# Sending the normalised rows of one more batch to columns through DRAM, and building a parity mask from the identity, in a fused attention and gated MLP kernel

## The chip, the cores and the metric

The kernel runs on one core of one Trainium2 chip. The metric is the time on the device in microseconds (us), and the number that stands for a kernel is the median of its runs. Four runs of the kernel before are known: 311.81, 311.83, 313.54 and 314.72 us, median 312.69 us. One execution was taken by the hardware profiler; its own time is 311.81 us, and the span from its first to its last instruction is 310.1 us. The granted TensorE clock was 1.0 over the whole span.

Engines are written as the profile writes them: PE is TensorE (matrix products), DVE is VectorE, ACT is ScalarE, POOL is GpSimd, SP is SyncE, whose queue here issues DMAs and nothing else.

## The reference, cut to what matters

```python
B, H, S, D = 8, 8, 576, 64                        # float32 inputs
scores = q @ k.T / sqrt(D)                        # per batch and head
rel = pos[:, None] - pos[None, :]
plain = (rel >= 0) & (rel < 32)                   # heads 0 to 3
dil = (rel >= 0) & (rel < 128) & (rel % 4 == 0)   # heads 4 to 7
attn = softmax(where(mask, scores, -1e9)) @ v
x = attn.transpose(0, 2, 1, 3).reshape(4608, 512) # a row per token
h = x @ w_in                                      # 512 -> 2048
g = h * sigmoid(beta * h)                         # beta: one number per column
out = g @ w_out                                   # 2048 -> 512, float32
```

Attention is narrow: a query sees 32 keys, either its neighbours (plain heads) or every fourth position behind it (dilated heads). Nearly all the arithmetic is in the two big products of the MLP.

## The kernel before, in words

**The MLP.** The 4608 tokens are cut into 9 tiles of 512. For each tile and each of 16 blocks of 128 hidden columns, `slot_h` makes h with four products (L818), each 128x128 weights by up to 512 tokens; ACT takes a tanh of it (L825) and DVE gates it into `g_t` (L830), of which there are two, used in turn. `block` then makes 128 rows of the output with 16 products over `g_t` and `w_out_bf` (L850); ACT or DVE brings them from PSUM to `osb` (L867, L869; four buffers), and SP stores them (L875). A tile is 64 products of each kind. Tile 0 has its first four blocks cut in two at token 288, so it has 80 of L818.

**What a tile of the MLP needs.** L818 reads `xT`, the attention output with features down the partitions and tokens along the columns. Tile 0 reads batch 0's tokens alone, in two halves; tile 1 batches 0 and 1; tile 2 (tokens 1024 to 1535) needs both halves of batch 2, and tile 3 batches 2 and 3.

**Attention of one batch.** The steps have names, in the order of the strings FIRST and LATER (L157, L158): KD0 to QP1 turn k and q to columns by PE transposes (L427, L434; only for batches below DIRECT = 3, later ones come transposed by DMA, L417); S2, S3 are scores of the dilated heads (L638), T those of the last 16 positions of each residue, the tail (L612), S00 to S11 those of the plain heads (L672 or L697). ACT takes exponentials (L580) and POOL or DVE multiply by 0/1 masks (L584). In batch 0 most masks are added by PE instead (L631, L661, L664), but the tail is always multiplied, by `mask_t`. V20 to V31 (L734), U (the tail, L719) and V00 to V11 (L749) multiply by the values, in tiles `vd`, `vt_` and `vp`, each with a column of ones, so that the sum of the weights comes out beside the result. DVE then takes a reciprocal (L598) and multiplies (L599) into `xdm` (dilated), `xdt` (tail) or `xsp[j]` (plain, token half j). Those are the normalised rows: tokens down the partitions.

**From rows to columns, in two ways.** For batches below BY_DMA = 3 the steps X2, X3 (from `xdm` and `xdt`: 4 transposes of 128 columns, L772, and one of 64, L774, each) and X00, X10, X01, X11 (from `xsp`: 3 transposes of 96 columns each, L790) go through PE into PSUM, and ACT or DVE copies PSUM to `xT` (8 copies of 288 columns, L218 by its helper). From batch 3 on, `back_dma` (L450) has SP store the rows into a DRAM tile `x` (L457 from `xsp`, L464 from `xdm`, four of L470 from `xdt` for the second half) and read them back with a DMA that transposes, straight into `xT` (L484): no PE, no copy.

**What sets the order.** Every step is an `op` of a planner (class Plan, L35): it has the engines that may run it with a guessed duration for each, its dependences, a due time `vt`, and for DMAs a guess of transfer and latency. `run` simulates the engines with these guesses and, at each point, gives an engine the op of lowest `vt` among those that can start first; the program is written out in that order, so each engine's order is fixed before anything runs. Where PE would be idle for more than 300 ns of the plan's first 80 us, a dummy product (L962) is put in. A batch's ops are due about one tile ahead of the tile that needs them.

**The places that the change touches.** `t_parity` (L329) and `t_mask_t` (L337) build `mask_t`: POOL makes `odd_even`, a 0/1 pattern of even and odd partitions (L331, L332), and a band of ones in `mask_t` (L318, L319, L322); DVE reduces `odd_even` to two columns (L338) and multiplies the band by them (L341, twice). `make_identity` builds `ident_b` on POOL early on, and `ident_f` (L900) for the one transpose of beta (L904). `direct_vd` (L392) loads `vd` and the two tail tiles `vt_`, `direct_vp` (L385) loads `vp`; for batch 0 the due times are -8.5, -8.499, -8.498 and -8.4. All loads of values and weights are issued by POOL. `spread` (L566) copies `vd` into place; `normed` (L590) is the reciprocal and the multiplication.

Of the kernel before, what the change touches and what calls it, by code (L numbers as in the profile page):

```python
# [9 lines left out]
BF16 = mybir.dt.bfloat16  # L10
# [151 lines left out]
def kernel(  # L162
# [35 lines left out]
    ADDED = 1  # L198
    BY_DMA = 3
    SPLIT = 4  # L200
# [30 lines left out]
    mask_t = const([P, 2, 4, 2, UT], BF16, "mask_t")  # L231
    odd_even = const([P, 2, KTL], BF16, "odd_even")
    odd_even_1 = const([P, 2], BF16, "odd_even_1")
    zero = const([P, 256], BF16, "zero")
# [94 lines left out]
    def t_parity(e):  # L329

        nc.gpsimd.memset(odd_even[:], 0.0)  # L331
        nc.gpsimd.affine_select(out=odd_even[:], in_=odd_even[:], pattern=[[1, 2], [2, KTL]], base=0,  # L332
                                channel_multiplier=-1, compare_op=ALU.not_equal, fill=1.0)
        band(mask_t[:].rearrange("p c h r u -> p (c h) r u"), [[0, 8]], [(1, 2), (2, UT)],
             2 * WIN, -1, 1.0, 0.0)

    def t_mask_t(e):  # L337
        nc.vector.tensor_reduce(out=odd_even_1[:], in_=odd_even[:], op=ALU.max, axis=mybir.AxisListType.X)  # L338
        m = mask_t[:].rearrange("p c h r u -> p (c h) r u")
        for r in range(2):  # L340
            nc.vector.tensor_tensor(  # L341
                out=m[:, :, r], in0=m[:, :, r], op=ALU.mult,
                in1=odd_even_1[:, r:r + 1].unsqueeze(2).to_broadcast([P, 8, UT]))

# [5 lines left out]
    adds["P"] = plan.op([("POOL", 1250)], t_add_p, vt=-7.5)  # L350
    par = plan.op([("POOL", 1900)], t_parity, vt=-7.295)
    mask_tail = plan.op([("DVE", 750)], t_mask_t, [par], vt=-3)

# [16 lines left out]
    def load(queue, args, deps, vt, kb, rate=.4, issue=750, lat=1100):  # L370
        return plan.op(
            [(queue, issue)],
            lambda e: dma(queue, *args), deps, vt, dma=kb * 1024 / rate / 1000, lat=lat)
# [18 lines left out]
    def direct_vd(b, deps, vt, tdeps=()):  # L392
        src = v[b, 4:8].rearrange("h (t T) d -> t h (T d)", T=C)[0:P]
        out = [load("POOL", (vd16_of[b].rearrange("p h T d -> p h (T d)"), src), deps, vt, 512, .35)]
        for c in range(2):
            src = bass.AP(tensor=v.tensor, offset=v[b, 4].offset + ((P - WIN) * C + c) * D,
                          ap=[[2 * D, 2 * KTL], [S * D, 4], [1, D]])
            out.append(load("POOL", (vt_[b % 2][:, c, :, 0:D], src), list(tdeps), vt + .001 + .001 * c, 96, .2))
        return out
# [50 lines left out]
    def back_dma(b, j, vt_of, vdone):  # L450
# [3 lines left out]
        out = []  # L454
        for e_ in range(2):
            out.append(plan.op(
                [("SP", 500)], lambda e, e_=e_: nc.sync.dma_start(  # L457
                    out=plain[e_], in_=xsp[j][e_ * QT // 2:(e_ + 1) * QT // 2].rearrange("p a x h d -> p a (x h d)")),
                [vdone[0, j], vdone[1, j]], vt_of[f"X1{j}"], dma=600, lat=2000))
# [29 lines left out]
    def attention(b, ld, names, vts):  # L489
# [76 lines left out]
        def spread(e):  # L566
            copy(e, vd[kv][:, :, :, 0:D], vd16_of[b])
        o = plan.op([("POOL", 1100), ("DVE", 850)], spread,
                    [ld["vd"][0], (fill3, fill4)[kv]] + war(("vd", kv)), vt)
# [20 lines left out]
        def normed(key, vop, g, vt, n, blocks, pv, dst, war_key):  # L590
# [4 lines left out]
            def norm(e):  # L595
# [5 lines left out]
                                        op=ALU.mult)  # L601
            vdone[key] = plan.op([("DVE", 400 + 1.042 * blocks * D)], norm, [vop] + war(war_key), vt - .003, group=g)

# [296 lines left out]
    def t_identf(e):  # L900
        make_identity(nc, ident_f[:])
    idf = plan.op([("POOL", 300)], t_identf, vt=-1.5)
    gb = Group("a")
# [92 lines left out]
```

## Time and profile before

| what | us |
|---|---|
| median of the runs shown | 312.69 |
| profiled execution, its own time | 311.81 |
| its span | 310.1 |
| PE busy (share of the span) | 302.0 (97%) |
| DVE busy | 193.0 (62%) |
| ACT busy | 173.9 (56%) |
| POOL busy | 104.1 (34%) |
| first product of the MLP (L818) starts | 20.47 |
| first L818 of tiles 1, 2 and 3 starts | 54.17, 82.19, 124.18 |
| last product of L850 starts | 304.5 |

Read it so. PE's busy time covers pipelined instructions that overlap, so 97% does not mean that nothing can be taken from PE; how close PE is to full is read from the distance between the starts of successive products. Four products of 512 columns take 0.86 us from start to start where they run without a break. The first 20 us are another world: attention of batch 0 runs alone, and PE mostly waits.

The DMA engines are busy at nine tenths or more from about 8 to 70 us and in several stretches later. SP's queue waits most of its time for output rows to store.

### The profile page before, as it was taken

To read this page: it belongs to the slowest core of one execution; us is meant where nothing else is said; L and a number is where in the kernel's file an instruction comes from. 1 tells how busy PE (TensorE), PEld (TensorE's weight loads), DVE (VectorE), ACT (ScalarE), POOL (GpSimd) and SP (SyncE) were. 2 spreads that over 40 slices of the span, in tenths; PEclk is the share of its full clock that TensorE was granted. 3 is DMA by queue.
4 is the path that set the end of the run, shared out by engine and by line. 5 is a ranking of instruction groups with operands and counts; after the bars stand their busy time and mean duration, and the time that the engine had idled before them with its cause. 6 is when DMAs were issued, how large, how long until landed. Compare 5 with 4: busy or idle time off the path is not lost.

```text
span 310.1 us, 6126 instructions
## 1 busy us (share of the span) xinstructions
PE 302.0 (97%) x2332; PEld 155.7 (50%) x2332; DVE 193.0 (62%) x422; ACT 173.9 (56%) x310; POOL 104.1 (34%) x153
## 2 busy tenths in 40 slices
PE   8899999999999999999999999999999999999995
PEld 5566546455455545444455455545544444444453
DVE  2587987797886756776866577776863443434300
ACT  2667866857565563665665557554753645455411
POOL 8999773523551506117535160143000000000000
PEclk9999999999999999999999999999999999999999
DMA  6999999998499855997999689993014400000121
GB/s 97 175 211 207 200 192 192 246 155 137 77 166 148 207 120 107 184 196 189 201 158 167 170 146 172 181 192 97 28 45 118 72 34 34 36 34 34 42 96 68
DMA packets 89920, 41.30 MB, mean 133 GB/s; under 512 B 68563, under 2 KB 84579, under 8 KB 89571
## 3 DMA queue, kind: packets, MB, share of 16 engines
q0 software_dynamic: 42336, 19.66, 52.7%
q1 hardware_dynamic: 47410, 21.19, 32.3%
q8 instruction: 18, 0.29, 0.4%
q14 instruction: 12, 0.09, 0.1%
q10 hardware_dynamic: 144, 0.07, 0.1%
HBM read 39.32 MB, written 18.28 MB: 186 GB/s over the span
## 4 chain that ended last, share of the span: by engine, by line
PE 88%; DVE 3%; DMA 2%; POOL 2%; ACT 2%; issue 2%; POOLq 0%; ACTq 0%
PE bank L850 39%; PE bank L818 39%; DMA raw<-in_v_dram 2%; PE bank L697 2%; PE bank L749 2%; PE bank L734 1%; POOL st L368 1%; PE bank L638 1%; PE bank L719 1%; ACT tnh L825 1%; PE bank L672 1%; PE bank L790 1%; ACT pt L580 1%; PE bank L612 1%; DVE g L830 1%
## 5 line engine op out<-in xcount | busy, mean ns | idle before, releaser
L825 ACT ACTIVATE tnh<-bank,beta_half 128x512 bf16<-128x512 f32 (+2 forms) x148 | 99.9, 677 | 87.9 <-PE bank L818 85.8
L830 DVE SCALAR_TENSOR_TENSOR g<-tnh,bank 128x512 bf16<-128x512 bf16 (+2 forms) x148 | 98.7, 671 | 76.9 <-ACT tnh L825 76.0
L850 PE MATMUL bank<-w_out_bf,g 128*128 128x512 bf16 (+1 forms) x592 | 143.7, 373 | 0.0
L818 PE MATMUL bank<-xT,w_in_bf 128*128 128x512 bf16 (+2 forms) x592 | 142.9, 373 | 0.6 <-DVE g L830 0.4
L818 PEld LDWEIGHTS <-w_in_bf 128*128 128x128 bf16 x592 | 54.9, 98 | 57.4 <-issue 1.1
L850 PEld LDWEIGHTS <-g 128*128 128x128 bf16 x592 | 54.3, 98 | 54.8
L867 ACT ACTIVATE osb<-bank 128x512 f32<-128x512 f32 (+2 forms) x36 | 21.0, 582 | 24.3 <-PE bank L850 23.3
L580 ACT ACTIVATE pt<-bank 128x384 bf16<-128x384 f32 (+1 forms) x54 | 22.8, 456 | 6.2 <-PE bank L697 2.8
L218 POOL COPY kz<-raw 64x1152 bf16<-64x1152 bf16 x6 | 9.6, 1601 | 28.4 <-DMA raw<-s 26.0
L580 ACT ACTIVATE ptd<-bank 128x512 bf16<-128x512 f32 x32 | 16.9, 602 | 3.2 <-PE bank L638 3.2
L599 DVE TENSOR_TENSOR xsp<-bank,rcp 96x384 bf16<-96x384 f32 x32 | 17.7, 554 | 1.1
L598 DVE RECIPROCAL rcp<-bank 128x4 f32<-128x4 f32 (+2 forms) x72 | 12.9, 179 | 4.7 <-PE bank L749 2.4
L599 DVE TENSOR_TENSOR xdm<-bank,rcp 128x256 bf16<-128x256 f32 x32 | 13.6, 424 | 1.1
L584 POOL TENSOR_TENSOR ptt<-ptt,mask_t 96x256 bf16<-96x256 bf16 x6 | 4.2, 695 | 29.8 <-ACT ptt L580 29.8
L584 DVE TENSOR_TENSOR ptd<-ptd,mask_d 128x512 bf16<-128x512 bf16 x27 | 11.8, 466 | 2.8 <-ACT ptd L580 2.5
L368 POOL DMA_DIRECT2D vp<-in_v_dram x9 | 12.0, 1334 | 1.2 <-DMA vp<-in_v_dram 1.2
L749 PEld LDWEIGHTS <-pt 128*128 128x128 bf16 x192 | 9.2, 97 | 6.0 <-DVE pt L584 0.7
L368 POOL DMA_DIRECT2D vt<-in_v_dram x16 | 10.9, 687 | 1.1 <-DMA w_out_bf<-in_moe_w_out_dram 1.1
L697 PEld LDWEIGHTS <-kz 128*128 128x128 bf16 x120 | 7.9, 98 | 6.0
L749 PE MATMUL bank<-vp,pt 128*128 128x65 bf16 x192 | 10.4, 193 | 0.1
L869 DVE TENSOR_SCALAR osb<-bank 128x512 f32<-128x512 f32 (+1 forms) x2 | 1.0, 492 | 13.8 <-ACT osb L867 13.7
L697 PE MATMUL bank<-qd,kz 128*128 128x96 bf16 x120 | 9.5, 206 | 0.0
(126 smaller groups left out, 223.6 us busy)
## 6 DMA issues: line engine op xcount, KB each, us to landing
out_dram<-osb SPq DMA_DIRECT2D x35, 256.0 KB, 3.1
s<-in_k_dram POOLq DMA_DIRECT2D x5, 576.0 KB, 6.3
s<-in_q_dram POOLq DMA_DIRECT2D x5, 576.0 KB, 9.8
vp<-in_v_dram POOLq DMA_DIRECT2D x7, 384.0 KB, 13.4
w_out_bf<-in_moe_w_out_dram POOLq DMA_DIRECT2D x2, 1024.0 KB, 15.6
st<-in_k_dram POOLq DMA_DIRECT2D x6, 288.0 KB, 13.0
st<-in_q_dram POOLq DMA_DIRECT2D x6, 288.0 KB, 13.4
x<-xsp SPq DMA_DIRECT2D x20, 72.0 KB, 2.4
```

The costliest lines, as they stand in the source:

```text
L368: {"POOL": nc.gpsimd, "SP": nc.sync}[queue].dma_start(out=out, in_=in_)
L580: nc.scalar.activation(out=w(), in_=sc(), func=ACT.Exp, scale=SCALE)
L584: E[e].tensor_tensor(out=w(), in0=w(), in1=m(), op=ALU.mult)
L598: nc.vector.reciprocal(out=r, in_=p[..., D])
L599: nc.vector.tensor_tensor(out=dst, in0=p[..., 0:D], in1=r.unsqueeze(len(p.shape) - 1).to_broadcast(list(p.shape[:-1]) + [D]), op=ALU.mult)
L697: nc.tensor.matmul(sc[:, a, h2 * QT:h2 * QT + QT], lhsT=kz[:, 2 * x + h2, i * QT:i * QT + P], rhs=qd[:, 2 * x + h2, :, i * QT // 2:(i + 1) ...
L749: nc.tensor.matmul(pv[:, a, h2, :], lhsT=pt[x][:, (3 * j + a) * 2 + h2], rhs=vp[kv][:, (2 * x + h2) * NI + 3 * j + a, 0:D + 1], start=True ...
L818: nc.tensor.matmul(bank(g)[:, 0:n], lhsT=w_in_bf[:, kt, fb * P:(fb + 1) * P], rhs=xT[:, kt, xo:xo + n], start=(kt == 0), stop=(kt == NKT - 1))
L825: nc.scalar.activation(out=th[:, 0:n], in_=bank(g)[:, 0:n], func=ACT.Tanh, scale=beta_half[:, fb:fb + 1])
L830: nc.vector.scalar_tensor_tensor(out=g_t[t % 2][:, fb, c0:c0 + n], in0=th[:, 0:n], scalar=1.0, in1=bank(g)[:, 0:n], op0=ALU.add, op1=ALU.mult)
L850: nc.tensor.matmul(bank(g)[:, lo:hi], lhsT=g_t[t % 2][:, fb, tb * P:(tb + 1) * P], rhs=w_out_bf[:, fb, lo:hi], start=(fb == 0), stop=(fb = ...
L867: nc.scalar.mul(out=ob[:, cols], in_=bank(g)[:, cols], mul=0.5)
```

## The change

Four things are done:

1. BY_DMA goes from 3 to 2, so batch 2 too takes `back_dma`. Since its plain queries are not split into even and odd ones as those of later batches are, its plain rows are stored by one DMA for each half instead of two.
2. The parity of the tail mask comes from the identity matrix: DVE reduces `ident_b` (columns seen as pairs) to two columns with a maximum, copies them over `mask_t`, and POOL then cuts the band out of that with two selects. `odd_even`, its memset and select, the memset of `mask_t` and DVE's two multiplications go away. The DVE part is due at -7.9, the POOL part at -7.295.
3. The tail's values are due behind the plain ones for batches 0 to 2: for batch 0 at -8.349 and -8.348 instead of ahead of -8.4, for batches 1 and 2 by 0.02 later, which is behind `vp` as well.
4. `ident_f` is due at -7.4 instead of -1.5, and the planner's guesses for DVE's `spread` (850 to 620 ns) and `norm` (400 to 310 ns before the part by size) are lowered.

```diff
@@ -196,7 +196,7 @@
     DV = 80
     DIRECT = 3
     ADDED = 1
-    BY_DMA = 3
+    BY_DMA = 2
     SPLIT = 4
 
     pool = lambda name, bufs: ctx.enter_context(tc.tile_pool(name=name, bufs=bufs))
@@ -229,8 +229,7 @@
     mask_n = {n: const([P, 2, 2, QT], BF16, f"maskn_{n}") for n in ("FP", "PP")}
     mask_d = const([P, 4, P], BF16, "mask_d")
     mask_t = const([P, 2, 4, 2, UT], BF16, "mask_t")
-    odd_even = const([P, 2, KTL], BF16, "odd_even")
-    odd_even_1 = const([P, 2], BF16, "odd_even_1")
+    parity = const([P, 2], BF16, "parity")
     zero = const([P, 256], BF16, "zero")
     warm = const([P, 1], FP32, "warm")
 
@@ -327,20 +326,21 @@
         band(add_d[:], [], [(1, P)], 0, WIN - 1, 0.0, NEG)
 
     def t_parity(e):
-
-        nc.gpsimd.memset(odd_even[:], 0.0)
-        nc.gpsimd.affine_select(out=odd_even[:], in_=odd_even[:], pattern=[[1, 2], [2, KTL]], base=0,
-                                channel_multiplier=-1, compare_op=ALU.not_equal, fill=1.0)
-        band(mask_t[:].rearrange("p c h r u -> p (c h) r u"), [[0, 8]], [(1, 2), (2, UT)],
-             2 * WIN, -1, 1.0, 0.0)
+        nc.vector.tensor_reduce(out=parity[:], in_=ident_b[:].rearrange("p (k r) -> p r k", r=2), op=ALU.max,
+                                axis=mybir.AxisListType.X)
+        nc.vector.tensor_copy(out=mask_t[:].rearrange("p c h r u -> p (c h) r u"),
+                              in_=parity[:].unsqueeze(1).unsqueeze(3).to_broadcast([P, 8, 2, UT]))
 
     def t_mask_t(e):
-        nc.vector.tensor_reduce(out=odd_even_1[:], in_=odd_even[:], op=ALU.max, axis=mybir.AxisListType.X)
+
         m = mask_t[:].rearrange("p c h r u -> p (c h) r u")
-        for r in range(2):
-            nc.vector.tensor_tensor(
-                out=m[:, :, r], in0=m[:, :, r], op=ALU.mult,
-                in1=odd_even_1[:, r:r + 1].unsqueeze(2).to_broadcast([P, 8, UT]))
+        step = [[0, 8], [1, 2], [2, UT]]
+        nc.gpsimd.affine_select(
+            out=m, in_=m, pattern=step,
+            base=2 * WIN, channel_multiplier=-1, compare_op=ALU.is_ge, fill=0.0)
+        nc.gpsimd.affine_select(
+            out=m, in_=m, pattern=[[-a, n] for a, n in step],
+            base=-1, channel_multiplier=1, compare_op=ALU.is_ge, fill=0.0)
 
     def t_add_p(e):
         band(add_p["P"][:], [], [(1, QT)], WIN, -1, 0.0, NEG)
@@ -348,8 +348,8 @@
         nc.gpsimd.memset(add_p["F"][0:WIN], NEG)
     adds = {"D": plan.op([("POOL", 900)], t_add_d, vt=-8.96)}
     adds["P"] = plan.op([("POOL", 1250)], t_add_p, vt=-7.5)
-    par = plan.op([("POOL", 1900)], t_parity, vt=-7.295)
-    mask_tail = plan.op([("DVE", 750)], t_mask_t, [par], vt=-3)
+    par = plan.op([("DVE", 600)], t_parity, [ident], vt=-7.9)
+    mask_tail = plan.op([("POOL", 1150)], t_mask_t, [par], vt=-7.295)
 
     def t_late(e):
         band(mask_d[:], [[0, 4]], [(1, P)], 0, WIN - 1, 1.0, 0.0)
@@ -395,7 +395,7 @@
         for c in range(2):
             src = bass.AP(tensor=v.tensor, offset=v[b, 4].offset + ((P - WIN) * C + c) * D,
                           ap=[[2 * D, 2 * KTL], [S * D, 4], [1, D]])
-            out.append(load("POOL", (vt_[b % 2][:, c, :, 0:D], src), list(tdeps), vt + .001 + .001 * c, 96, .2))
+            out.append(load("POOL", (vt_[b % 2][:, c, :, 0:D], src), list(tdeps), vt + (.15 if b == 0 else .02 if b < DIRECT else 0) + .001 + .001 * c, 96, .2))
         return out
 
     scratch = {}
@@ -452,7 +452,13 @@
         rows = dram_pool.tile([S // 2, HD], BF16, name=f"x{b}_{j}")
         plain = rows[:, 0:HD // 2].rearrange("(i m e) c -> e m i c", e=2, m=QT // 2)
         out = []
-        for e_ in range(2):
+        if b < DIRECT:
+            out.append(plan.op(
+                [("SP", 500)], lambda e: nc.sync.dma_start(
+                    out=rows[:, 0:HD // 2].rearrange("(i m) c -> m i c", m=QT),
+                    in_=xsp[j][:].rearrange("p a x h d -> p a (x h d)")),
+                [vdone[0, j], vdone[1, j]], vt_of[f"X1{j}"], dma=1200, lat=2000))
+        for e_ in range(2 if b >= DIRECT else 0):
             out.append(plan.op(
                 [("SP", 500)], lambda e, e_=e_: nc.sync.dma_start(
                     out=plain[e_], in_=xsp[j][e_ * QT // 2:(e_ + 1) * QT // 2].rearrange("p a x h d -> p a (x h d)")),
@@ -565,7 +571,7 @@
         vdeps["P"] = ld["vp"] + [(fill3, fill4)[kv]]
         def spread(e):
             copy(e, vd[kv][:, :, :, 0:D], vd16_of[b])
-        o = plan.op([("POOL", 1100), ("DVE", 850)], spread,
+        o = plan.op([("POOL", 1100), ("DVE", 620)], spread,
                     [ld["vd"][0], (fill3, fill4)[kv]] + war(("vd", kv)), vt)
         used("vd16" if b < DIRECT else ("st", kv), o)
         wrote(("vd", kv))
@@ -599,7 +605,7 @@
                 nc.vector.tensor_tensor(out=dst, in0=p[..., 0:D],
                                         in1=r.unsqueeze(len(p.shape) - 1).to_broadcast(list(p.shape[:-1]) + [D]),
                                         op=ALU.mult)
-            vdone[key] = plan.op([("DVE", 400 + 1.042 * blocks * D)], norm, [vop] + war(war_key), vt - .003, group=g)
+            vdone[key] = plan.op([("DVE", 310 + 1.042 * blocks * D)], norm, [vop] + war(war_key), vt - .003, group=g)
 
         for name in [n for n in names if n[0] in "ST"]:
             vt = vt_of[name]
@@ -899,7 +905,7 @@
 
     def t_identf(e):
         make_identity(nc, ident_f[:])
-    idf = plan.op([("POOL", 300)], t_identf, vt=-1.5)
+    idf = plan.op([("POOL", 300)], t_identf, vt=-7.4)
     gb = Group("a")
     bt = plan.op([("PE", 300)], lambda e: nc.tensor.transpose(bank(gb)[:, 0:NFB], beta_row[:, :], ident_f[:, :]),
                  [beta_ld, idf], -1.4, acquire=gb)
```

## The prediction, as put on record

> **What bounds the kernel now.** I read the page first (its busy table and 40 slices), then the timeline of PE, then that of the first 21 us with the chain of waits, then the landings of the tiles that the change loads or writes.
>
> The page, busy us and slices:
>
> ```profile
> PE 302.0 (97%) x2332; PEld 155.7 (50%) x2332; DVE 193.0 (62%) x422; ACT 173.9 (56%) x310; POOL 104.1 (34%) x153
> PE   8899999999999999999999999999999999999995
> DMA  6999999998499855997999689993014400000121
> ```
>
> PE is the engine to watch, and slice 10 (77.5 to 85.3 us) is the one early stretch with free DMA engines. The timeline of PE (start, us, op, count) shows what "busy" is worth where batch 2 turns its rows:
>
> ```profile
> 70.77 0.39 PE L772 MATMUL bank<-ident_b,xdm 128*128 128x128 bf16 x4
> 71.09 0.20 PE L774 MATMUL bank<-ident_b,xdt 64*128 64x64 bf16 x1
> ...
> 71.69 0.30 PE L790 MATMUL bank<-ident_b,xsp 96*128 96x96 bf16 x3
> 71.82 1.03 PE L850 MATMUL bank<-w_out_bf,g 128*128 128x512 bf16 x4
> ...
> 80.11 0.29 PE L790 MATMUL bank<-ident_b,xsp 96*128 96x96 bf16 x3
> 80.24 1.03 PE L850 MATMUL bank<-w_out_bf,g 128*128 128x512 bf16 x4
> ...
> 82.19 1.03 PE L818 MATMUL bank<-xT,w_in_bf 128*128 128x512 bf16 x4
> ```
>
> Start to start there is no hole: four 512-column products take 0.86 us (0.2158 each), and from 54 us to the end almost all work starts when the one before lets it. So past 54 us, what leaves PE leaves the kernel, and other engines are free of charge until PE runs out of ready work. The last line is tile 2's first L818, just after batch 2's last copy (81.53 + 0.40).
>
> The first 20 us are different. The timeline there (idle before and its releaser in brackets):
>
> ```profile
> 12.99 0.23 DVE L338 TENSOR_REDUCE odd_even<-odd_even 128x2 bf16<-128x96 bf16 x1
> 13.51 0.52 POOL L322 TENSOR_SCALAR_AFFINE_SELECT mask_t<-mask_t 128x256 bf16<-128x256 bf16 x1
> 14.07 0.49 DVE L341 TENSOR_TENSOR mask_t<-mask_t,odd_even 128x128 bf16<-128x128 bf16 x2 [0.85 <-POOL mask_t L322]
> 14.48 0.17 DVE L598 RECIPROCAL rcp<-bank 128x4 f32<-128x4 f32 x1
> 15.17 0.20 PE L661 MATMUL bank<-add_F,ident_b 128*128 128x96 bf16 x1 [0.56 <-DVE xdm L599]
> 15.72 1.42 ACT L580 ACTIVATE pt<-bank 128x288 bf16<-128x288 f32 x4 [0.59 <-PE bank L672]
> 19.52 0.23 PE L904 MATMUL bank<-ident_f,beta_row 16*128 16x16 f32 x1 [0.18 <-POOL ident_f masks.py:199]
> 20.47 0.77 PE L818 MATMUL bank<-xT,w_in_bf 128*128 128x288 bf16 x5 [0.27 <-ACT xT L218]
> ```
>
> DVE sits 0.85 us behind POOL's mask while V20's result, done at 13.5, waits for its reciprocal; PE waits for a bank that DVE holds, ACT for PE. The chain runs through these very pieces, and later through POOL's queue to `ident_f` and the beta transpose.
>
> **Part 1: batch 2 off PE.** Removed: 4+1+4+1 transposes for X2, X3 and 3 for each of four X steps, 22 in all. Start to start they take 0.92 (70.77 to 71.69), then 0.13, 0.13 (73.55), 0.13 and 0.14 (81.19): 1.45 us; the chain, which counts the hand-overs, books 1.52. I take 1.5. All of it is in the stretch without holes: 1.5 us gained if nothing new opens. Eight copies go too (ACT six, DVE two, about 0.4 us each); they are beside PE and I count nothing. Added on SP, ten DMAs: two L457, two L464 (0.86 each), four L470 (0.46) and two L484 (1.30). The single plain store is twice the size of any shown, so between 0.43 and 0.86 of issue; I take 0.6. Sum 1.2 + 1.7 + 1.8 + 2.6 = 7.3 us in 70 to 90 us, where SP otherwise issues three output stores. SP is in order, so a transposing DMA that waits for its store (L484 waited 8.5 us once, between 125 and 155 us) holds the output stores behind it; those have four `osb`, 4 x 4 x 0.86 = 13.8 us of L850. No PE hole followed that 8.5 us.
>
> When does tile 2 get its `xT`? The tiles `xsp` and `xT` (issue to landing):
>
> ```profile
> DMA to landing us min/median/max: 1.8/2.4/3.8
> DMA to landing us min/median/max: 3.6/4.4/7.0
> ```
>
> Batch 2's last multiplication ends at 81.13 (80.58 + 0.55). Store and transpose make that 81.13 + 2.4 + 4.4 = 87.9, at worst 81.13 + 3.8 + 7.0 = 91.9, against 81.93 now. The plan's own guesses (0.5 + 0.9 + 1.2 + 2.0, then 1.3 + 0.9 + 1.5 + 3.5) add 11.8 and place tile 2 near 93, up to 2.7 more where it charges for POOL's queue. PE's cover: before 82.19 the timeline has 68 L850 of the 128 of tiles 0 and 1, so 60 are left, 60 x 0.2158 = 12.9 us, to 95.1, plus some 2 us of batch 3's scores and values that now lie between. The delay fits, with little to spare against the plan's pessimism. What waits for the read of `xdm` and `xdt`: batch 3's first multiplication, at 87.35; the stores issue from about 70 and the slowest landing of an `xdt` store is 10.4, so about 82. Batch 4's casts (from 81.19) share the DMA engines with the transposes; their first use is at 113.67.
>
> The Trainium skill ("VectorE: DVE Perf Modes", Rules for kernel authors) speaks against this part: a 128x128 transpose belongs on TensorE where PSUM will do. Its table gives 390 ns there and 1309 by the DMA crossbar; by that my estimate for 18 such squares is 7.0 against 23.6 us, later than the cover of 12.9, a loss of some 10 us. The rows decide otherwise: 22 transposes cost PE 1.45 us, and L484 lands half a batch in 4.4.
>
> **Part 2: mask and parity.** DVE adds a reduction of 128 columns (0.23 for 96, so 0.23 to 0.31) and one copy of 256 (0.28 for 128 to 0.49) near 3.5 us, when it has nothing to do until dk at 6.95: free. POOL loses 12.00 to 12.86 (odd_even and memset) and keeps two selects, which end near 13.6, before ptt's exponential ends at 14.53. DVE loses L338 and L341, 0.72 us, and the wait, so V20's reciprocal moves from 14.48 to about 13.55. What is late next is ACT, busy to 15.12: its idle 0.59 before 15.72 and 0.24 before 17.38 are what can close. **`ident_f`** built before the first w_in load costs POOL 0.4 us there against 0.9 saved, so later DMA issues move up by 0.5; their landings follow the full DMA queue and stay. PE's 0.35 us stop before L904 goes.
>
> **Part 3: tail values behind the plain ones.** Landings by issue plus time: `vd` 12.44, `vt_` 12.8 and 13.2, `vp` 16.3 and 16.7, w_in 18.9. They come in order of issue, so `vp` moves up by the 0.76 of the two, to 15.5 and 15.9, and `vt_` goes to 16.7. V00, at 17.28, can start near 16.2. U, at 16.32, moves to 16.7; its multiplication ends at 17.9 instead of 17.49, X2 starts at 18.0 (17.94 now), X3 ends at 18.8, the copies at 19.2. So the first L818 goes from 20.47 to about 19.3: 1.15 us for parts 2 and 3 together. Ends: no better than w_in's 18.9 (1.5), and nothing if the tail lands as slowly as the slowest row (9.75 + 8.5 = 18.3, then U 0.4, DVE 0.6, X3 0.5, copies 0.8: 20.6). I take 1.15, since landings in a full queue go by its order. In batches 1 and 2 the same swap brings V00 forward and U back; PE has L850 or L818 to do there: nothing.
>
> **Part 4: guesses.** They move no instruction by themselves, but each engine's order may change. DVE's vd copies measured 0.42 to 0.60 and POOL's 1.10, the norm 0.74 for 384 columns: the new guesses are nearer. Bound: PE's holes between 20.4 and 45 us, about 3 us in the timeline, can close or grow by 1 us. I take zero.
>
> **Sum.** 311.81 - 1.5 - 1.15 = 309.2 for the profiled execution. That stands 0.9 below the median, so 312.7 - 2.6 = **310.1**.
>
> **Rivals.** *More* (0.20): earlier DVE and fewer copies also close half of the 3 us of holes and the 0.4 us that PE stood at 77.6 to 78.2: 308.0, between 306.8 and 309.5. For it: those holes wait for DVE and ACT. Against: some wait for loads. *Less* (0.20): batch 1's loads land when they do, and the ramp's 1.15 us come back as holes between 28 and 41 us: only part 1 is left, 311.2 (310.5 to 312.2). For it: `st` holds PE at 28.19, and the DMA slices are full. Against: L818 of tile 0 is ready work until 47. *Slower* (0.12): tile 2's order stands ahead of what lands. From 97 us (82.19 + 12.9 + 2) each us of lateness is a us of PE; at the plan's worst plus a store held 8.5 us on SP it is about 6, less the 2.6: 316 (313 to 319). Against: 91.9 is the worst sum of rows. *Does nothing* (0.03): both gains are eaten by the new order, 312.5.
>
> **How the numbers follow.** The likeliest, 0.45, has its own range of 309.0 to 311.2. 1% of 312.69 is 3.1 us, about what a measurement of this kernel can tell from no change. Faster by over 1% (under 309.6) are all of *more* and a third of the likeliest: 0.35. Slower by over 1% (over 315.8) is two thirds of *slower*: 0.08. Within: 0.57. The range 307.3 to 313.0 leaves out the low end of *more* (0.03) and nearly all of *slower* (0.11).
>
> **What would show it.** Right: no L772, L774, L790 of batch 2; first L818 at 19.0 to 19.6; no wait of DVE on mask_t; V00 of batch 0 before 16.6; tile 2's first L818 at 90 to 97 with unbroken L850 before it. Wrong: a hole in PE before that L818, a first L818 after 20.2, U's multiplication later than 18.2, or holes of more than 4 us between 20 and 45.

## The result and the profile after

| kernel | median us (lowest to highest) | runs | ratio to before (95% interval) |
|---|---|---|---|
| before, beside it | 313.39 (311.81 to 318.05) | 61 | |
| changed | 311.57 (310.42 to 312.77) | 40 | 0.9947 (0.9933 to 0.9961) |

The change takes about 1.7 us away (0.53%; by the interval 1.2 to 2.1). Forecast were 310.1 us and 2.6 us less: the direction is right, the change stays within 1% as was held likeliest, and the gain was forecast too large by half. The ratio leaves out runs that were disturbed as a whole; but 21 of the 61 runs of before are over 314 us and none of the changed kernel's, so a part of the 1.7 us is this spread: from lowest to lowest the change is worth 1.4 us. The profiled execution of the changed kernel took 312.34 us, among the longest of its runs, while that of before (311.81) was the shortest of its own; so below the two traces are compared by places, not by their ends.

The page of the changed kernel (busy us, then the slices):

```profile
PE 300.1 (97%) x2307; PEld 153.9 (50%) x2307; DVE 200.9 (65%) x421; ACT 171.2 (55%) x302; POOL 108.9 (35%) x150
PE   8899899999999999999999999999999999999994
DMA  6999999999789975999999869997024100101112
```

PE has 25 instructions less, the 22 transposes and three fillers, and ACT 8 less. DVE is the surprise: one instruction less, and 7.9 us more of busy time. If each instruction is counted at the fastest instance of its kind (operation, tiles, shape) in any of the traces, and the times are added up, DVE's work is 1.1 us less than before; what comes on top of that, its *excess*, went from 12.9 to 22.8 us. So the instances are slower.

The ramp, timeline of the changed kernel (start, us, engine, line, op, out<-in, count):

```profile
3.44 0.29 DVE L329 TENSOR_REDUCE parity<-ident_b 128x2 bf16<-128x128 bf16 x1 [1.03 <-POOL ident_b masks.py:199]
3.76 0.42 DVE L331 COPY mask_t<-parity 128x256 bf16<-128x256 bf16 x1
13.87 0.17 DVE L604 RECIPROCAL rcp<-bank 128x4 f32<-128x4 f32 x1
15.84 0.36 PE L755 MATMUL bank<-vp,pt 128*128 128x65 bf16 x6
16.61 0.44 PE L725 MATMUL bank<-vt,ptt 96*64 96x65 bf16 x8
17.36 0.42 DVE L605 TENSOR_TENSOR xdt<-bank,rcp 64x256 bf16<-64x256 f32 x1
18.92 0.67 DVE L218 COPY xT<-bank 128x288 bf16<-128x288 bf16 x2 [0.37 <-PE bank L780]
19.64 1.14 PE L824 MATMUL bank<-xT,w_in_bf 128*128 128x288 bf16 x8 [0.27 <-DVE xT L218]
```

The parity lies in DVE's empty time, no wait for `mask_t` is left ahead of the reciprocal (13.87 for 14.48), V00 (now L755) starts at 15.84 instead of 17.28, and the first product of the MLP (now L824) at 19.64 instead of 20.47. U (L725) starts at 16.61 and its multiplication ends at 17.78, as the prediction had them (16.7 and 17.9). The new last link is in the seventh line: two copies to `xT` one behind the other on DVE.

Tile 2, timeline of PE in the changed kernel:

```profile
77.29 1.03 PE L856 MATMUL bank<-w_out_bf,g 128*128 128x512 bf16 x4
78.95 1.02 PE L856 MATMUL bank<-w_out_bf,g 128*128 128x512 bf16 x4 [0.64 <-DVE g L836]
...
89.55 1.02 PE L856 MATMUL bank<-w_out_bf,g 128*128 128x512 bf16 x4
90.42 6.85 PE L824 MATMUL bank<-xT,w_in_bf 128*128 128x512 bf16 x31
```

Its first product comes at 90.42, within the forecast 90 to 97, and waits for nothing: the rows that now go by DRAM are there in time. But at 78 us there is a hole that was not there before: PE waits for DVE's gate. The other lines say what DVE did:

```profile
74.06 3.00 POOL L218 COPY kz<-raw 64x1152 bf16<-64x1152 bf16 x2
75.91 2.27 DVE L218 COPY qt<-dq 64x128 bf16<-64x128 bf16 x2
76.98 1.15 POOL L218 COPY qd<-raw 64x1152 bf16<-64x1152 bf16 x1
78.21 0.69 DVE L836 SCALAR_TENSOR_TENSOR g<-tnh,bank 128x512 bf16<-128x512 bf16 x1
```

Two small copies of 64x128, which took 0.19 us each on DVE in the kernel before, take 2.27 together. The first ends at 77.12, 0.05 after POOL's second `kz` (77.07), the other at 78.18, 0.05 after POOL's `qd` (78.13). The gate at 78.21 stands behind them, though the tanh that it reads had ended at 76.45. In the kernel before, these two were POOL's. The groups by shape, before and after (count, then busy us and mean ns), show that this is wider than one place:

```profile
L218 DVE COPY qt<-dq 64x128 bf16<-64x128 bf16 x4 | 0.8, 191 | 0.1
L218 DVE COPY qd<-raw 64x1152 bf16<-64x1152 bf16 x13 | 5.9, 452 | 0.2
```

```profile
L218 DVE COPY qt<-dq 64x128 bf16<-64x128 bf16 x11 | 6.1, 551 | 0.7 <-DMA dq<-s 0.4
L218 DVE COPY qd<-raw 64x1152 bf16<-64x1152 bf16 x14 | 11.0, 788 | 0.2
```

The Trainium skill ("SBUF — State Buffer", section "SBUF: two separate sides") says that DVE, in a performance mode that uses two ports, and GpSimd share one pair of ports, that whichever instruction starts first holds it to its end, and that the other engine is blocked meanwhile. The two copies, each of which ends 0.05 us after the copy of POOL that began ahead of it, agree with that.

Last, the end of the span. From the last compute instruction (DVE's copy to `osb`) to the end are 2.59 us before and 3.81 after; the last compute instruction itself ends 0.68 us earlier than before (306.83 for 307.51). The closing sequence waits for the completion semaphores one by one, in a fixed order. SP's DMAs, and one store that ACT issues, take eight of them in turn. SP issued 118 DMAs before and 128 after, so the last store moved by two places in that round, from number 117 to 108. The trace's events on SP, us behind the last compute instruction:

```
wait passed     106   108   112   113   114   115   116   117   118   111
before          0.41  0.46  0.52  0.58  0.65  1.09  1.43  1.61  1.67  1.74
changed         0.40  1.71  1.78  2.17  2.26  2.32  2.38  2.45  2.51  2.57
```

Before, the wait for the last store is nearly the last one, and the others lie within the store's flight. After, it is the second, and the rest, some 0.07 each and one stop of 0.39, come behind it.

### The profile page after: what moved, and what is told of

Same layout as the page of the kernel before. It is cut to its first block, busy times and chain, and to the rows that moved or that the text cites. A ratio compares the mean times of both kernels' runs of the same rounds, so it can differ in the third digit from the quotient of the medians.

```text
span 310.6 us, 6066 instructions
## 1 busy us (share of the span) xinstructions
PE 300.1 (97%) x2307; PEld 153.9 (50%) x2307; DVE 200.9 (65%) x421; ACT 171.2 (55%) x302; POOL 108.9 (35%) x150
## 4 chain that ended last, share of the span: by engine, by line
PE 81%; POOL 5%; DMA 5%; DVE 5%; issue 1%; ACT 1%; POOLq 0%; ACTq 0%; DVEq 0%
PE bank L856 36%; PE bank L824 35%; DMA raw<-in_v_dram 5%; PE bank L755 2%; PE bank L703 2%; PE bank L740 2%; DVE qd L218 1%; POOL st L368 1%; PE bank L725 1%; PE bank L644 1%; DVE g L836 1%; DVE qt L218 1%; POOL kz L362 1%; PE bank L678 1%; DVE kz L218 0%
## 5 line engine op out<-in xcount | busy, mean ns | idle before, releaser
L824 PE MATMUL bank<-xT,w_in_bf 128*128 128x512 bf16 (+2 forms) x592 | 141.5, 373 | 0.4 <-DVE xT L218 0.3
L856 PE MATMUL bank<-w_out_bf,g 128*128 128x512 bf16 (+1 forms) x592 | 141.1, 373 | 0.6 <-DVE g L836 0.6
L856 PEld LDWEIGHTS <-g 128*128 128x128 bf16 x592 | 55.4, 98 | 58.7 <-issue 0.9
L824 PEld LDWEIGHTS <-w_in_bf 128*128 128x128 bf16 x592 | 55.1, 98 | 58.2 <-issue 0.8
L586 ACT ACTIVATE pt<-bank 128x384 bf16<-128x384 f32 (+1 forms) x54 | 22.0, 455 | 6.1 <-PE bank L703 3.5
L218 POOL COPY vd<-st 128x1024 bf16<-128x1024 bf16 x4 | 4.4, 1093 | 31.2 <-DMA st<-in_v_dram 31.2
L590 POOL TENSOR_TENSOR pt<-pt,maske_FP 128x384 bf16<-128x384 bf16 x7 | 6.3, 912 | 21.4 <-ACT pt L586 13.4
L755 PEld LDWEIGHTS <-pt 128*128 128x128 bf16 x192 | 9.1, 97 | 6.1 <-DVE pt L590 0.7
L218 DVE COPY qd<-raw 64x1152 bf16<-64x1152 bf16 x14 | 11.0, 788 | 0.2
L755 PE MATMUL bank<-vp,pt 128*128 128x65 bf16 x192 | 10.4, 193 | 0.6 <-DVE pt L590 0.6
## 6 DMA issues: line engine op xcount, KB each, us to landing
st<-in_k_dram POOLq DMA_DIRECT2D x6, 288.0 KB, 12.9
```

What stands on the lines that cost most here:

```text
L218: (nc.scalar.copy if e == "ACT" else E[e].tensor_copy)(out=out, in_=in_)
L586: nc.scalar.activation(out=w(), in_=sc(), func=ACT.Exp, scale=SCALE)
L590: E[e].tensor_tensor(out=w(), in0=w(), in1=m(), op=ALU.mult)
L755: nc.tensor.matmul(pv[:, a, h2, :], lhsT=pt[x][:, (3 * j + a) * 2 + h2], rhs=vp[kv][:, (2 * x + h2) * NI + 3 * j + a, 0:D + 1], start=True ...
L824: nc.tensor.matmul(bank(g)[:, 0:n], lhsT=w_in_bf[:, kt, fb * P:(fb + 1) * P], rhs=xT[:, kt, xo:xo + n], start=(kt == 0), stop=(kt == NKT - 1))
L856: nc.tensor.matmul(bank(g)[:, lo:hi], lhsT=g_t[t % 2][:, fb, tb * P:(tb + 1) * P], rhs=w_out_bf[:, fb, lo:hi], start=(fb == 0), stop=(fb = ...
```

## One ledger for the traces

To see where time comes from, I count PE's idle time up to a moment: the moment less the products done by then, each at 0.4167 ns a column and 2.5 ns, which makes the 0.2158 us of a 512-column product in an unbroken run, fillers not counted. The table is that idle time less the kernel before's (minus: less idle), for executions whose traces hold all of PE's records (those of e1 to e4 lack some). The last columns are differences too. Time that PE loses in passing from one shape of product to another counts as idle here.

| kernel | 20.6 us | 60 | 90 | 125 | 220 | work of PE | last product | end behind last compute | span |
|---|---|---|---|---|---|---|---|---|---|
| changed | -0.73 | -1.35 | -1.34 | -1.56 | +0.45 | -1.02 | -0.68 | +1.21 | +0.5 |
| changed, again (e8) | -0.37 | -0.36 | -0.45 | -0.91 | +0.37 | -1.02 | -0.75 | +1.21 | +0.5 |
| e10, old guesses | -0.61 | -0.27 | -0.76 | -1.13 | -0.88 | -1.02 | -1.85 | +0.83 | -1.0 |
| e11, six loads more | +0.12 | -0.69 | -0.90 | -1.13 | -0.88 | -1.02 | -1.94 | +0.46 | -1.5 |
| e6, part 3 alone | +0.24 | -0.49 | -0.49 | -0.86 | -0.69 | 0 | -0.79 | 0 | -0.8 |
| e5, part 2 alone | -0.74 | -0.36 | +0.77 | +1.30 | +1.46 | 0 | +1.52 | 0 | +1.5 |
| e9, copies on DVE | -0.24 | -0.58 | -1.12 | -0.75 | +3.00 | -1.02 | +1.95 | +0.93 | +2.9 |
| e7, batch 1 too | -0.37 | +0.40 | +9.99 | +11.33 | +11.24 | -2.03 | +9.50 | +0.27 | +9.8 |
| e12, before and two loads | 0 | -0.03 | 0 | -0.22 | 0 | 0 | +0.04 | +0.52 | +0.6 |

Executions of one order agree to 0.2 us up to 220 us in one case (before and e12), and differ by up to 1.0 in the other (the first two rows at 60 us). So a difference of less than 1 us between two rows, each of one execution, is weak evidence. Row by row, span is last product plus end.

## The experiments

The theory after the result: the transposes were worth about what was forecast; the ramp gave less, because the tail values land later than assumed; and some of it is given back by slower DVE copies and by the longer end. The main rival: that DVE beside POOL costs most of what is missing. The runs bear the theory out in part: the tail values were late in some executions only.

### One part at a time

**e1**, part 1 alone (batch 2 through DRAM, with the single plain store for each half, which is not shown), on the kernel before:

```diff
-    BY_DMA = 3
+    BY_DMA = 2
```

> Part 1 alone: batch 2's rows go by DRAM and DMA transposes, mask, tail loads and guesses as before. Theory: PE loses 1.5 us of transposes in a stretch without holes, and a part of that comes back as a new PE hole near 78 us, where tile 2 is not ready and PE is left with output products that wait for DVE's gates (0.8 us in the profile after). So 0.5 to 1.5 us faster than before, first MLP product still at 20.4 to 20.5. Rival (PE had slack there anyway): within 0.3 us of before.

Measured: 311.03 us (310.55 to 312.5), ratio 0.994 (0.9909 to 0.9971). The first product is at 20.45 as before, the last one of the kernel 1.61 us earlier, and the end is already on semaphore 108, 0.83 us longer. The hole that was expected near 78 us is not there. So part 1 alone gives as much as the whole.

**e4**, the kernel before with batch 2's 22 transposes issued twice, in the same order:

```diff
-                    for c in range(C):
+                    for c in [*range(C)] * (2 if b == 2 else 1):
...
-                for a in range(3):
+                for a in [*range(3)] * (2 if b == 2 else 1):
```

> The kernel before, same order of everything, with each of batch 2's 22 PE transposes issued twice. Theory (PE full there, 1.45 us of transposes is worth 1.45 us): 1.0 to 1.7 us slower than before. Rival (slack on PE): within 0.3 us of before.

Measured: 313.08 us (312.8 to 319.29), ratio 1.0007 (0.9972 to 1.0041); its lowest is 1.0 above the lowest of before (311.81). The ratio can't tell this from no change; the lowest times, and the trace in this stretch, speak for 1.0. At the ledger's price the 22 are 1.02 us of work. In the trace ten transposes more in X2 and X3 lengthen the way from the first L772 to the first L790 from 0.91 to 1.42 us, while the products around them come 0.216 apart as before. The steps into and out of the shape of L774 (0.15 and 0.13 us, against 0.056 from one L772 to the next) do not double with them. So doubling shows the work alone, 1.0; the 1.45 read from start to start holds 0.4 of such steps besides, and these go too when the transposes go. e1's 1.61 fits 1.45.

**e2**, the change without part 1:

```diff
-    BY_DMA = 2
+    BY_DMA = 3
```

> The changed kernel with batch 2 back on PE transposes (parts 2 to 4 only). Theory: the first MLP product stays at 19.6, 0.8 us before its old place, and PE keeps this to the end since tile 0 has ready work to 47 us: 0.5 to 1.2 us faster than before. Rival (the ramp's gain is given back while batch 1's loads land): first product at 19.6, tile 1's first at 54 again, time within 0.3 us of before.

Measured: 311.47 us (310.45 to 312.02), ratio 0.9951 (0.9923 to 0.9979). The time is right, the reason was not: the first product is at 20.40, not near 19.6. U was spread over 17.07 to 17.81, waiting for its values, which landed 7.6 to 8.3 us behind their issue; and it began 0.46 later than in the changed kernel's profile, because `vd` had landed at 13.17 instead of 12.83.

**e5**, part 2 with `ident_f` alone, and **e6**, part 3 alone, which moves the tail values of batches 1 and 2 as well (both on the kernel before):

```diff
-    par = plan.op([("POOL", 1900)], t_parity, vt=-7.295)
-    mask_tail = plan.op([("DVE", 750)], t_mask_t, [par], vt=-3)
+    par = plan.op([("DVE", 600)], t_parity, [ident], vt=-7.9)
+    mask_tail = plan.op([("POOL", 1150)], t_mask_t, [par], vt=-7.295)
...
-    idf = plan.op([("POOL", 300)], t_identf, vt=-1.5)
+    idf = plan.op([("POOL", 300)], t_identf, vt=-7.4)
```

> The kernel before with the tail mask's parity from the identity alone (part 2; batch 2's rows through TensorE, the tail values loaded where they were, the old guesses). First theory (in the ramp DVE's wait for the mask is what the change takes away, and the tail values' late landing then gives part of it back): without the moved load DVE's reciprocal comes at 13.5 to 13.9 instead of 14.48 but the plain values land where they did, so that the first MLP product comes at 19.9 to 20.45. Rival (the mask alone set the ramp): 19.3 to 19.8. Time by either 311.0 to 312.4, the last store on the old semaphore and the end 2.6 to 2.9 us long.

```diff
-list(tdeps), vt + .001 + .001 * c, 96, .2))
+list(tdeps), vt + (.15 if b == 0 else .02 if b < DIRECT else 0) + .001 + .001 * c, 96, .2))
```

> The kernel before with batch 0's tail values loaded behind the plain ones alone (part 3). First theory: DVE still waits for the mask, the plain values land some tenths earlier and the tail values later; the first MLP product stays at 20.2 to 20.6, and later by up to 0.5 us if the tail values then end the ramp. Rival (the plain values' landing set the ramp): 19.6 to 20.1. Time 311.8 to 312.8 by the first, 311.0 to 311.6 by the second.

Measured: e5 314.18 us (313.35 to 318.59), ratio 1.0045 (1.0013 to 1.0078); e6 311.31 (310.63 to 315.45), ratio 0.9945 (0.9912 to 0.9978). Neither is as expected. e5 has the early first product (19.65, the rival's figure: the mask alone set the ramp's end) and is 1.5 us slower than before; e6 has the late one (20.60, the first theory's figure) and is faster. The ledger says why. Of e5's 0.74 us in hand at 20.6, half is gone at 60, and then one place costs more than all of it. DVE, POOL and PE of e5:

```profile
77.89 2.42 POOL L218 COPY qd<-raw 64x1152 bf16<-64x1152 bf16 x2
78.03 2.33 DVE L218 COPY qt<-dq 64x128 bf16<-64x128 bf16 x2
81.22 0.55 DVE L599 TENSOR_TENSOR xsp<-bank,rcp 96x384 bf16<-96x384 f32 x1
81.83 0.30 PE L790 MATMUL bank<-ident_b,xsp 96*128 96x96 bf16 x3 [1.40 <-DVE xsp L599]
```

It is the place of 78 us again: the new order has DVE make the `qt` copies, POOL's `qd` copies hold them for 2.33 us (80.36 against 80.31 for POOL's end), and `xsp`, which PE waits for, comes behind. In the kernel before they are on POOL (77.65, 0.70 for both), and in e6 and e10 too (1.19 and 0.62). In the changed kernel's two executions and in e11 the stop is 0.6 to 0.8 us; in e10, where POOL makes the `qt` copies, there is none.

**e3**, part 4's two guesses for DVE alone, on the kernel before, and **e10**, the change without them:

```diff
-("DVE", 850)
+("DVE", 620)
-("DVE", 400 + 1.042 * blocks * D)
+("DVE", 310 + 1.042 * blocks * D)
```

> Only the planner's two guesses (DVE spread 850 to 620, norm 400 to 310), no work added or removed. Theory: they reorder engines and nothing else, within 0.7 us of before either way. Rival: they put more DVE copies beside POOL copies, which then take two to three times as long; DVE's busy time rises by 3 us or more over 193.0 and the kernel is 0.5 to 1.5 us slower than before.

> The changed kernel with the planner's old guesses (850 and 400). The guesses alone made the kernel before about 0.5 to 1 us faster. Theory (what each part gains alone is partly the same thing, a plan that is less fragile than that of before): within 0.7 us of the changed kernel. Rival (the guesses' gain is there in the sum and the other parts bring the rest): 0.5 to 1 us slower than the changed kernel.

Measured: e3 311.91 us (311.33 to 312.72), ratio 0.9966 (0.9939 to 0.9994); e10 311.27 (310.72 to 312.02), 0.9933 (0.99 to 0.9966), where the changed kernel, run again beside it as e8, had 311.85 (311.0 to 312.38) and 0.9937 (0.9901 to 0.9973). So the rival, 0.5 to 1 us slower without the new guesses, falls; the old ones are if anything better, by 0.6 us in the median of these two sets of 12 runs, and by 0.3 against all runs of the changed kernel.

> The changed kernel unaltered, for a second profile, since its first one was among the slowest of its runs. Theory: the places of the holes between 125 and 220 us (2.1 us there in the first profile) stay, their sizes move with DMA landings; first MLP product between 19.6 and 20.4, by when the tail's values land (the same order in another kernel gave 20.40). Rival: the holes are an accident of one execution and are gone.

The profile of e8 has 1.3 us between 125 and 220 us, the most of it at one place where the first profile had none (below); the places do not stay. Its first product is at 20.10, within the expected range, but not by the tail's values: they landed at 16.29 and 16.47, and `vd` at 13.20.

The parts do not add: 0.6% (e1), 0.5% (parts 2 to 4), 0.34% (part 4) and 0.55% (part 3) alone, 0.45% lost by part 2 alone, and 0.53% gained together. Each part reorders much of the first 90 us, and part 1 lengthens the end.

### DVE beside POOL

**e9**, the change with all `kz` and `qd` copies on DVE, so that POOL's long copies are gone:

```diff
-    o = plan.op([("POOL", 1200), ("DVE", 1400)], spread, [ld["x", 0, 0], late_fill] + war("kz"), vt)
+    o = plan.op([("DVE", 850)], spread, [ld["x", 0, 0], late_fill] + war("kz"), vt)
...
-    o = plan.op([("DVE", 900)] + ([("POOL", 1150)] if half == e_ else []), spread,
+    o = plan.op([("DVE", 480)], spread,
```

> The changed kernel with the copies of k and q into kz and qd (batches 3 to 7) on DVE alone, guesses 850 and 480 ns as measured, none on POOL. Theory (the change's plan lets POOL's and DVE's copies overlap, DVE's then take two to three times as long and PE waits for the gate or mask behind them): DVE's excess over its own fastest instances falls from 17.7 us to under 9, the holes of 0.8 at 78 us and of 2.1 between 125 and 220 us shrink by half or more, 0.5 to 2 us faster than the changed kernel. Rival (DVE just becomes the busier engine): same time or slower, with holes in other places.

Measured: 315.27 us (314.6 to 316.03), ratio 1.0054 (1.0022 to 1.0086), 3.4 above the changed kernel beside it. Without POOL's copies DVE has more to do: its work, each instruction at its fastest, is 5.7 us more than in e8, and its excess is 17.6 us against 20.2, far from the half that was expected; POOL still multiplies masks and copies values there. Between 125 and 220 us PE idles 3.75 us more. So e9 says that DVE can't take POOL's copies at no cost, and leaves open what the collisions cost as such. On that e10 says more: its excess is 18.5 us, 5.6 above that of the kernel before, and its PE idles 0.88 us less by 220 us. What costs is where a blocked copy stands ahead of something that PE needs, not how many there are.

### How far part 1's cover reaches

**e7**, the change with batch 1 through DRAM as well:

```diff
-    BY_DMA = 2
+    BY_DMA = 1
```

> The changed kernel with BY_DMA = 1: batch 1 too goes by DRAM. It tests the cover. In the profile after, tile 1 starts at 52.65 with 28 output products of tile 0 in hand, 6.0 us, and a row's way through DRAM adds 7 to 10 us to its readiness while the DMA engines are full, so PE runs dry: 1.5 us of transposes saved, 2 to 6 us of holes at 52 to 62 us, 0.5 to 4 us slower than the changed kernel. Rival (a transfer of this kind is hidden wherever it stands): another 0.7 to 1.5 us faster.

Measured: 321.32 us (319.07 to 322.22), ratio 1.0225 (1.0165 to 1.0285). Two lines of its PE timeline:

```profile
63.58 0.89 PE L725 MATMUL bank<-vt,ptt 96*64 96x65 bf16 x8 [2.98 <-DMA vt<-in_v_dram]
71.43 1.89 PE L824 MATMUL bank<-xT,w_in_bf 128*128 128x512 bf16 x8
```

Tile 1 starts at 71.43 instead of 52.7, with all of tile 0's products used up. Another 1.02 us of transposes saved costs 9 to 10 us. PE's two longest stops are 2.98 us in the first line, for values that land, and 4.05 at 90.32, where tile 2's first product waits for batch 2's own rows from DRAM (`DMA xT<-x`): the delay of tile 1 has used up batch 2's cover as well. The same edit pays for batch 2 while output products of tiles 0 and 1 cover it, and loses for batch 1, which has no such cover.

### The end

**e11**, the change and six loads of 512 bytes that nothing uses, issued on SP ahead of all; **e12**, the kernel before and two:

```diff
+    spare = const([1, 6, P], FP32, "spare")
+    for i in range(6):
+        nc.sync.dma_start(out=spare[:, i], in_=moe_beta.rearrange("(f p) -> f p", p=P)[i:i + 1, :])
     plan.run(filler, 80000.0)
```

> The changed kernel whole, and six loads of 512 bytes each (rows of beta, into a tile that nothing reads) issued on SP ahead of everything else, so that SP issues 134 DMAs instead of 128 and its last store falls on the same one of the eight completion semaphores (117) as in the kernel before (118 DMAs); the order of all other work is unchanged. Theory (the closing sequence waits for the semaphores in a fixed order, and the last store of the changed kernel is on the first of those waits, so that all others come behind it): from the last compute instruction to the end of the span 2.6 to 2.9 us instead of 3.4 to 3.8, and the time 0.7 to 1.2 us below the changed kernel's. Rival (the longer end comes from the ten transfers themselves, or from chance): 3.4 to 3.8 us and the changed kernel's time within 0.3 us.

> The kernel before, and two loads of 512 bytes (rows of beta, read by nothing) issued on SP ahead of everything else: 120 DMAs, and the last store on semaphore 108 as in the changed kernel. Theory: from the last compute instruction to the end of the span 3.4 to 3.8 us instead of 2.59, and the lowest times 0.7 to 1.2 us above the kernel before's. Rival: 2.6 us, and its lowest times within 0.3 us of the kernel before's.

Measured: e11 310.60 us (309.61 to 311.37), ratio 0.992 (0.9885 to 0.9955); e12 312.67 (312.27 to 313.44), ratio 0.999 (0.996 to 1.0021), its lowest 0.5 above that of before (311.78). The last store was on 117 in e11 and on 108 in e12, as meant. SP's events again, the last wait and then the span's end, us behind the last compute instruction:

```
                     store on   last wait passed   end of span
before               117        1.74               2.59
e11                  117        1.83               3.05
e12                  108        2.15               3.11
changed              108        2.57               3.81
```

So the direction holds both ways, and the size was half wrong. The order of the waits is worth 0.41 us (2.15 against 1.74). The rest of the 1.2 are single stops of 0.3 to 0.4 us in the closing sequence: one in e11, two in the changed kernel, none in the profile of before. e2, whose last store is on 117, has such a stop too (an end 0.30 longer than before). The trace has one or two transfers of 8 KB on an instruction queue near them; whether these are the cause wasn't tried. e11's median is 1.0 below the changed kernel's (from other sets of runs), and the end of its profile 0.76 shorter. It is the fastest kernel of the study.

## Why the prediction was right or wrong

**What bounds it: right.** What leaves PE leaves the kernel: without the 22 transposes e1's last product came 1.61 us earlier, and doubling them made the lowest time 1.0 longer. In e10 and e11 0.88 us less idle time at 220 and 1.02 us less work make 1.90, and the last product came 1.85 and 1.94 earlier.

**Part 1: right.** 1.5 was taken; 1.02 us of PE's work went (ledger, e4) with some 0.4 of steps between shapes, and the last product of e1 came 1.61 earlier. The cover held: tile 2 at 90.42 against 90 to 97, no wait for `xT`. The ten DMAs did not hold the output stores up. The estimate that the prediction made from the Trainium skill's table ("VectorE: DVE Perf Modes", section "The three transpose paths": 390 ns on TensorE, 1309 by DMA), and set aside for the rows' own, would have been wrong by its sign here. For the batch before (e7) its sign is right, by the missing cover.

**Parts 2 and 3: right mechanism, the term mis-sized.** The wait for the mask went, the parity cost nothing, V00 came before 16.6. But 1.15 us of gain at the first product were 0.83, 0.37, 0.67 and -0.06 (changed kernel, e8, e10, e11). Three steps of the sum were off. The first is "the copies at 19.2", 0.4 us behind the end of X3: two copies to `xT` stand one behind the other on DVE there (0.67 us, shown above), and in all four executions the first product starts 0.83 us behind X3 instead of 0.5. This alone makes 19.64 of 19.3. The second is the start: `vd` was taken to land at 12.44 as before, and landed at 12.83, and at 13.20 in e8:

```profile
13.22 0.53 DVE L218 COPY vd<-raw 128x1024 bf16<-128x1024 bf16 x1 [1.74 <-DMA raw<-in_v_dram]
```

There V20 starts 0.46 us later than in the first profile (13.80 for 13.34), and the first product as much. The third is "landings in a full queue go by its order". The tail values, issued at 8.4 and 9.1, landed 7.1 to 8.4 us later, against 6.0 to 6.3 before, issued at 6.5 and 7.2. In three of the four executions they were there by the forecast 16.7; in e11 the second landed at 17.51, and PE waited in the midst of U:

```profile
16.51 0.22 PE L725 MATMUL bank<-vt,ptt 96*64 96x65 bf16 x1
17.55 0.38 PE L725 MATMUL bank<-vt,ptt 96*64 96x65 bf16 x7 [0.83 <-DMA vt<-in_v_dram]
20.53 1.14 PE L824 MATMUL bank<-xT,w_in_bf 128*128 128x288 bf16 x8 [0.27 <-DVE xT L218]
```

That is the low end that the prediction worked out (20.6) and did not choose. And e5 shows that the moved load was not needed for the ramp's end: with the mask alone it came at 19.65.

**The first product was the wrong place to measure.** Its time missed the stated 19.0 to 19.6 in all four executions, and in e8 and e11 the tail's multiplication ended behind the 18.2 that was to show a mistake (18.24 and 18.67). But it does not say what the ramp is worth: e6 is 0.13 us later there and 0.86 better at 125. In all executions with part 2 or 3 in the ledger PE idles 0.3 to 0.7 us less between 20.6 and 25 us, at the fillers and gates of tile 0's first blocks, which the prediction did not look at; but in e3, where only guesses changed and the ramp stayed, it is 0.7 too, so this belongs to the new order and not to the ramp. At 125 us the changed kernel's two executions, e10 and e11 have 0.9 to 1.6 us in hand. That is near the 1.15 forecast, but it holds the 0.4 of part 1's steps between shapes and what other orders bring, so no run shows how much of it is the ramp's.

**The rival *Less* was partly right.** In e5 half of the ramp's gain is given back before 60 us, as it said. In the changed kernel's two executions, e10 and e11 what is left there varies between 0.27 and 1.35.

**Part 4: inside its bound of 1 us, but not for nothing.** Guesses or not, each edit to the first 90 us is free to move others: in the changed kernel as in e5, which has the old guesses, DVE took over the `qt` copies of batch 3, and PE got a hole, of 0.6 to 0.8 us in the changed kernel, near 78 us, which e10 (the old guesses) and e1 do not have. The prediction's own sign of being wrong, "a hole in PE before that L818", came true, for a reason that it had not named: not a store or a transpose, but a small copy blocked behind POOL ahead of the gate.

**The end was in no step.** The ten added DMAs were priced at 7.3 us of SP's time and hidden. They cost 0.4 us by turning the last store to an early semaphore. The end was up to 1.2 longer with the stops that came along, whose cause is open.

**What stays open.** In two executions of the changed kernel, 1.3 and 2.0 us of idle time came back between 125 and 220 us, at places that differ (147, 175, 198 us in one, 212 in the other); in e11, whose order is the same but for six loads at the start, 0.25. So the order alone does not make it. At each of the four PE waits for DVE, and there DVE had stood beside POOL. The largest of the first profile, and the same mask product in e8, where PE has no stop:

```profile
196.50 1.04 POOL L218 COPY vd<-st 128x1024 bf16<-128x1024 bf16 x1 [9.29 <-DMA st<-in_v_dram]
196.53 1.23 DVE L590 TENSOR_TENSOR pt<-pt,maske_PP 128x384 bf16<-128x384 bf16 x1
197.81 0.30 PE L755 MATMUL bank<-vp,pt 128*128 128x65 bf16 x4 [0.56 <-DVE pt L590]
```

```profile
196.18 0.35 DVE L590 TENSOR_TENSOR pt<-pt,maske_PP 128x384 bf16<-128x384 bf16 x1
197.02 1.04 POOL L218 COPY vd<-st 128x1024 bf16<-128x1024 bf16 x1 [10.15 <-DMA st<-in_v_dram]
```

In e11 POOL's copy begins at 195.24, overlaps a part of the product, and this takes 0.74. POOL's copy starts when a load lands, so here it is the landing that decides whether the two meet. Whether all of the 1.3 and 2.0 us comes about so is not shown, nor why the landings differ.

## What to carry to other kernels

Where a planner writes the order, cost an edit's new neighbours as well: a copy of 0.2 us that moves to DVE beside a long copy on POOL costs up to POOL's whole copy, and only matters if something that PE needs is queued behind it. Value a shorter ramp not at the first product but at a point where PE has run without holes for a while. When a change adds DMAs, look where the last store's completion stands among the closing waits; a few spare DMAs can move it.

## What was not expected of the hardware

Two copies of 64x128 on DVE took 2.27 and 2.33 us together beside POOL's copies, against 0.19 each, and each ended 0.05 us after one of POOL's did, in two kernels. The closing sequence passed one semaphore each 0.06 to 0.07 us once nothing was left to land, so an early wait for the last store cost 0.41 us. In e7, with PE idle for long stretches, the granted clock fell to 0.94 over 52 to 92 us, where the changed kernel had 1.0:

```profile
52.00:92.00 40.00, 31.13 (x278) 15.82 (x277) 22.19 (x48) 18.76 (x35) 10.25 (x14) 0.94 1.27 163
```

(the stretch, then busy us and instructions of PE, weight load, DVE, ACT and POOL, the clock, the DMA share and GB/s). After the stops of 2.98 and 4.05 us the 512-column products came up to 0.43 us apart instead of 0.216; over both places that is 2.3 us of e7's loss.
